# Gated attention with a squared-ReLU MLP: squares, sums and low parts on other engines, a new order of operations in the MLP stage

## The chip, the cores and the metric

The kernel runs on one core of one Trainium2 chip. The metric is the device time of one execution in microseconds (us); lower is better. The core's engines are TensorE (PE, with its weight loads PEld), VectorE (DVE), ScalarE (ACT), GpSimd (POOL) and SyncE (SP, which here only issues DMAs). Each engine takes its own instructions in order and waits for others by semaphores.

## The reference

```python
x = A_x                                # 2048 x 640
xn = _layernorm(x, axis=-1)
s = _A_ref(xn, k_cache, v_cache, wq, wo)   # 32 heads of 128, the last 512 cached keys
g = _silu(_B_ref(xn, w1, b1, w2, b2))      # h = xn @ w1 + b1; r = max(h, 0); (r * r) @ w2 + b2
return x + s * g
```

The MLP's hidden width is 1728, which is 13 chunks of 128 and one of 64 (14 chunks, FC = 14). The model width of 640 is 5 chunks of 128 (DC = 5).

## The kernel before

All products are float32 products made of three TensorE passes: each operand is split into a high part `hi` (a rounded copy, written by ScalarE) and a low part `lo` = operand - hi (a subtraction), and `triple` adds hi\*hi, hi\*lo and lo\*hi into one PSUM bank. So each operand costs one ScalarE copy and one subtraction.

The 2048 tokens are four tiles of 512: tile 0, T1 = 1, T2 = 2 and LATE = 3. Everything is held transposed (model width on the partitions, tokens along the free axis). The program has these stages:

1. **First stage, 14 steps** (`first_step(f)`, about 12 to 118 us). Step f makes hidden chunk f of tile 0 (`up`: 15 matmuls), then its ReLU (ScalarE, `up_end`), its square and split (`square_split`), and then the down product of the chunk before (`down(f - 1)`, 15 matmuls into five PSUM banks). The weights of chunk f come by SP's queue two steps ahead (`load_part`), and are split by `split_w(f, k)`: k = 0 for w1, k = 1 for w2. Beside this, the steps prepare tiles T1 and T2: `ln_load` loads the rows of x, `ln_block` takes their statistics on VectorE, `ln_var` and `ln_root` make mean and reciprocal deviation, `ln_rows` turns them into rows (a TensorE transpose, a VectorE copy, a DMA to DRAM, and two DMAs that broadcast them back into the tiles `mr`), and `ln_chunk(t, c)` loads chunk c of x transposed, subtracts the mean, multiplies, and splits it into the tiles `xT`.
2. **The seven block products** (about 118 to 212 us). The up products of T1 and T2 are made for six pairs of hidden chunks. A pair is a 2 x 2 matrix of blocks (two hidden chunks by two parts of the width), the two tiles are the other one, and Winograd's form needs seven products (`PROD`) instead of eight. `t_sums` makes the sums of x (once), `w_sums(p)` those of the weights of pair p, and `w_split(p, k)` the splits of the weights. `w_first`, `w_second` and `w_third` issue the products of pair p; additions between PSUM banks happen on VectorE (tile `wy` = product sum + p5 in `w_second`, tile `wx` = a + p5 in `w_third`). The fifth chunk of the width is added by `rest`. Each finished chunk goes through `up_end` and `square_out` to DRAM (`h_m`).
3. **The down products of T1 and T2** (`c_load`, `c_prep`, `c_down`, 28 steps), beside which tile LATE is normalised by `ln_chunk`.
4. **Attention** (from about 316 us to the end), whose order is written out by hand with due times, and in which the MLP of tile LATE is placed.

What sets the order: the helper objects `pe`, `dve`, `act`, `pool` and `sp` keep each instruction in program order on its engine, and all of them have line 77 (L77) in the profile. Calls through `nc.vector`, `nc.gpsimd`, `nc.scalar`, `nc.sync` and `nc.tensor` are not kept in order: a planner places them where it expects their inputs to be ready. Such are, in the kernel before, the loads of x (L149, L212), the moves of the rows (L179 to L191), the whole of `ln_chunk` (L213 to L216) and `t_sums` (L535 to L540).

Pools of tiles: `xr` on the right side of SBUF holds `xT` of T1 and the sums `T` of x; `keep` holds `xT` of T2 under the tag acc. The raw weights lie in the tag wr (4 buffers) of pool `mx`, or, for chunks not divisible by three below 9, in acc. Chunks of x lie in the tags stage and mr (2 buffers each) and xb (4). Results of ReLU lie in the tag r (4 buffers).

Of the kernel before, what the change touches and what calls it, by code (L numbers as in the profile page):

```python
# [10 lines left out]
AF = mybir.ActivationFunctionType  # L11
# [14 lines left out]
def kernel(  # L26
# [67 lines left out]
    def raw(ap):  # L94
        return ap.bitcast(F32)
# [105 lines left out]
        ]  # L201

    def ln_chunk(t, c):
        bc, xs = LN[t], XS[t]
        xc = (
            pa.tile([P, D], F32, tag="xb", name=f"xc{t}_{c}", bufs=NB)
            if t == T2 and c in (1, 3)
            else xp.tile(
                [P, D], F32, tag="mr" if t == T2 and c == DC - 1 else "stage", name=f"xc{t}_{c}"
            )  # L210
        )[:, :NT]
        nc.sync.dma_start(xc, xT[c * P : (c + 1) * P, t * NT : (t + 1) * NT])  # L212
        (nc.vector if t == T1 or t == T2 and c > 2 else nc.gpsimd).tensor_tensor(xc, xc, bc[0], op=ALU.subtract)  # L213
        (nc.gpsimd if t == LATE else nc.vector).tensor_tensor(xc, xc, bc[1], op=ALU.mult)
        nc.scalar.activation(xs[0][:, c, :], xc, AF.Copy)
        nc.vector.tensor_tensor(xs[1][:, c, :], xc, raw(xs[0][:, c, :]), op=ALU.subtract)  # L216
        XC[t, c] = xc

    PRE, BOTH, BR = {}, {}, []

# [164 lines left out]
    def split_lo(f, r, k, engine):  # L385
        hi, lo = split_parts(f, k)
        engine.tensor_tensor(lo, r, raw(hi), op=ALU.subtract)

    def split_w(f, k):
        if f < FC:  # L390
            split_hi(f, PRE[f, k], k)
            split_lo(f, PRE[f, k], k, pool if k and 5 <= f < 9 else dve)
            if 8 <= f < FC - 2:
                load_part(f + 2, k)

    def square_split(f, r, hi, lo):
        pool.tensor_tensor(r, r, r, op=ALU.mult)
        if f not in (0, rp, rp + 1) and f < AHEAD_W:
            split_w(f + 1, 0)
        act.activation(hi, r, AF.Copy)  # L400
        dve.tensor_tensor(lo, r, raw(hi), op=ALU.subtract)

    def square_out(t, f, r):
        pool.tensor_tensor(r, r, r, op=ALU.mult)
        sp.dma_start(h_m[t, f][: chunks[f][1], :], r)

    def r_tile(t, f):
# [64 lines left out]

    def up_end(t, f, ph):
        r = r_tile(t, f)
        if t == 0 and f == rp + 1:
# [54 lines left out]
    def t_sums(q):  # L530
        e, o = 2 * q, 2 * q + 1
        (h1, l1), b12, b22 = XS[T1], XC.pop((T2, e)), XC.pop((T2, o))
        t = [tmp(f"ts{q}_{k}") for k in range(4)]
        eng = nc.vector
        eng.tensor_tensor(t[0], b12, raw(h1[:, e, :]), op=ALU.subtract)  # L535
        eng.tensor_tensor(t[0], t[0], raw(l1[:, e, :]), op=ALU.subtract)
        eng.tensor_tensor(t[1], b22, t[0], op=ALU.subtract)
        eng.tensor_tensor(t[2], b22, b12, op=ALU.subtract)
        eng.tensor_tensor(t[3], raw(h1[:, o, :]), t[1], op=ALU.subtract)
        eng.tensor_tensor(t[3], t[3], raw(l1[:, o, :]), op=ALU.add)  # L540
# [19 lines left out]
    def w_sums(p):  # L560
        a, b = WR[p, 0], WR[p, 1]
        a11, a12, a21, a22 = (w[:, k : 2 * NQ2 : 2, :] for w in (a, b) for k in range(2))
        s = [
            (
                tmp(f"ws{p}_{k}")
                if p
                else xp.tile([P, NT], F32, tag="p5", name=f"ws{p}_{k}", bufs=2)
            ).rearrange("p (k q n) -> p k q n", k=2, n=P)
            for k in range(2)
        ]  # L570
        s1, s2, s3, s4 = (w[:, k] for w in s for k in range(2))
        pool.tensor_tensor(s1, a21, a22, op=ALU.add)
        pool.tensor_tensor(s2, s1, a11, op=ALU.subtract)
        pool.tensor_tensor(s3, a11, a21, op=ALU.subtract)
        pool.tensor_tensor(s4, a12, s2, op=ALU.subtract)
        SUMS["w", p] = s

    def wb(tag, shape, name):
# [83 lines left out]
            b[k] = ps_y.tile([P, NT], F32, tag="py", name=f"w{k}{p}")  # L662
        act.activation(b["x"], b["a"], AF.Copy)

    def w_second(p):
        b = PB[p]
        prod(p, 5, b["y"], True)
        b["p5"] = xp.tile([P, NT], F32, tag="p5", name=f"p5_{p}", bufs=2)
        act.activation(b["p5"], b["y"], AF.Copy)
        prod(p, 6, b["a"])  # L670
        dve.tensor_tensor(b["y"], b["a"], b["p5"], op=ALU.add)
        prod(p, 2, b["x"])
        rest(p, 0, 0, b["x"])
        up_end(T1, PAIRS[p][0], b["x"])

    def w_third(p, between=None):
# [12 lines left out]
        up_end(T2, PAIRS[p][1], b["x"])  # L689

    AHEAD_W = 6
    CH = {1: {7: (0, 1), 8: (2, 3), 9: (4,)}, 2: {9: (0,), 10: (1, 2), 11: (3, 4)}}

    def first_step(f):
        if f == 1:
            ln_load(T1)
        if f == 4:
            ln_load(T2)
        if f > 0:
            split_w(f, 1)  # L700
# [5 lines left out]
        for t in (T1, T2):  # L706
            for c in CH[t].get(f, ()):
                if c == 0:
                    open_x(t)
                ln_chunk(t, c)  # L710
# [12 lines left out]
        if f == 12:  # L723
            w_load(0)
        if f == 13:
            w_load(1)
            t_split(1)
        if f == 1:
            PY[0] = [ps_y.tile([P, NT], F32, tag="py", name=f"py0_{d}") for d in range(DC)]
        if f > 0:  # L730
            down(f - 1, home(f - 1, 1), HS.pop(f - 1), PY[0])
        if f == 12:
            t_sums(0)
            t_split(0)
            t_sums(1)

# [457 lines left out]
    down(FC - 1, home(FC - 1, 1), HS.pop(FC - 1), PY[0])  # L1194
    gate(0, gate_tile, range(2))
    up(T1, rp)
    gate(0, gate_tile, (2,))
# [11 lines left out]
    for p in range(1, NP):  # L1209
# [2 lines left out]
            w_load(p + 2)  # L1212
        w_first(p)
        w_seed(p)
        if more:
            w_sums(p + 1)
        w_third(p - 1)
        if more:
            w_split(p + 1, 0)
        else:  # L1220
            for k in range(2):
                c_prep(0, k)
        if p == 1:
            ln_load(LATE)
        if p in (2, 3):
            spill(p - 1, XS[p - 1])
            for b in range(2):
                ln_block(LATE, 2 * (p - 2) + b)
        if p == 3:
            ln_var(LATE)  # L1230
            LN[LATE] = ln_root(LATE)
        if p == NP - 2:
            for m in range(3):
                c_load(m)
        if p == 4:
            LN[LATE] = ln_rows(LATE, LN[LATE])
        w_second(p)
        if more:
            w_split(p + 1, 1)
            w_split(p + 1, 2)  # L1240
    up(T2, FC - 1)
    c_prep(1, 1)
    w_third(NP - 1)
    c_prep(1, 0)
    xctx.close()
    bctx.close()
    for m in range(2 * FC):
# [3 lines left out]
        if m + 2 < 2 * FC:  # L1251
            for k in range(2):
                c_prep(m + 2, k)
        c = m - 2
        if c == 0:
            open_x(LATE)
        if 0 <= c < DC:
            ln_chunk(LATE, c)
        if 0 < c <= DC:
            spill(LATE, XS[LATE], slice(c - 1, c))  # L1260
# [291 lines left out]
```

## Time and profile before

| | |
|---|---|
| time, median of 3 runs | 1977.48 us (1975.9 to 1977.9) |
| time of the profiled execution | 1977.58 us |
| its span | 1975.8 us |
| granted TensorE clock, mean of the span | 0.997 of full speed |
| busy: PE, DVE, POOL, ACT | 99%, 81%, 72%, 62% |
| start of attention's first score products | 316.44 us into the span |

How to read it: the page gives busy times and shares of the whole span, which is mostly attention. The stages that the change touches lie in its first 316 us; there the timeline (instructions in order of time: start, duration, engine, line, operation, `output<-inputs`, count, and in brackets the idle time before it and what ended it) is the view to read. A TensorE row's duration runs to the end of its last matmul and overlaps with the next row by about 0.16 us, so that the length of a group is read from start to start.

### The profile page before, as it was taken

What the parts mean: (1) busy time and instruction counts of PE and PEld (TensorE: products, weight loads), DVE (VectorE), ACT (ScalarE), POOL (GpSimd) and SP (SyncE); (2) the same over time, 40 slices, a digit from 0 to 9 for tenths busy, and PEclk for the clock granted to TensorE, in tenths of its full rate; (3) what the DMA queues carried; (4) which work ended last, traced back from release to release, by engine and by line L of the source; (5) the groups of instructions that cost most, each with busy time, mean ns of one, the idle gap of its engine ahead of it and who ended that gap; (6) DMA issues with size and microseconds to landing.
All of it is one profiled execution on the core that took longest, in us unless ns stands there. A gap on an engine that the chain in (4) does not pass through costs nothing.

```text
span 1975.8 us, 28654 instructions
## 1 busy us (share of the span) xinstructions
PE 1949.8 (99%) x8576; PEld 1605.6 (81%) x8576; DVE 1604.2 (81%) x2717; ACT 1225.4 (62%) x2122; POOL 1426.0 (72%) x798
## 2 busy tenths in 40 slices
PE   9898999999999999999999999999999999999998
PEld 7676887888888888888888888888888888888887
DVE  6865555788888888888888878888888888888864
ACT  5354444766666666666666676666666666666643
POOL 2355503888888888888888888888888888888841
PEclk9899999999999999999999999999999999999999
DMA  6547674333333322232335443433333333322253
GB/s 197 184 149 258 248 259 154 103 91 92 91 92 93 93 93 91 91 92 92 91 92 162 154 120 102 113 114 114 115 115 118 116 117 114 97 92 92 84 187 117
DMA packets 147640, 246.43 MB, mean 125 GB/s; under 512 B 25020, under 2 KB 47334, under 8 KB 146214
## 3 DMA queue, kind: packets, MB, share of 16 engines
q1 hardware_dynamic: 144486, 230.02, 37.3%
q0 software_dynamic: 2864, 14.42, 1.8%
q8 instruction: 77, 1.26, 0.2%
q14 instruction: 69, 0.57, 0.1%
q10 hardware_dynamic: 144, 0.16, 0.0%
HBM read 213.59 MB, written 30.95 MB: 124 GB/s over the span
## 4 chain that ended last, share of the span: by engine, by line
PE 92%; issue 3%; DVE 2%; DMA 1%; ACT 0%; SPq 0%; POOL 0%; ACTq 0%; DVEq 0%; POOLq 0%
PE r L77 22%; PE pq L77 22%; PE s L77 18%; PE o L77 18%; PE py L77 4%; PE ly L77 2%; PE ph L77 2%; PE lu L77 2%; PE wa L77 1%; PE wx L77 1%; PE wy L77 1%; PE eu L77 1%; DMA w1r<-in_w_dram 0%; DVE st L77 0%; DMA mv_d<-lr 0%
## 5 line engine op out<-in xcount | busy, mean ns | idle before, releaser
L77 POOL TENSOR_TENSOR pt<-e,pt 128x1024 fp32r<-128x1024 f32 x256 | 615.4, 2404 | 112.8 <-ACT pt L77 63.6
L77 PE MATMUL r<-ot,wo 128*128 128x512 f32 x1920 | 496.6, 389 | 0.0
L77 PE MATMUL pq<-ax,wq 128*128 128x512 f32 x1920 | 456.1, 389 | 0.0
L77 PEld LDWEIGHTS pq<-ax,wq 128*128 128x128 f32 x1920 | 360.3, 188 | 75.2 <-DVE q L77 0.4
L77 PEld LDWEIGHTS r<-ot,wo 128*128 128x128 f32 x1920 | 360.3, 188 | 74.9
L77 PE MATMUL s<-q,wk 128*128 128x512 f32 x1536 | 369.1, 389 | 0.9 <-DVE sgl L77 0.9
L77 PE MATMUL o<-pt,wv 128*128 128x512 f32 x1536 | 369.2, 389 | 0.0
L77 DVE TRANSPOSE_TENSOR_REDUCE rdm<-s 128x16 f32<-128x512 f32 x512 | 347.3, 712 | 6.2 <-PE s L77 6.1
L77 ACT ACTIVATE e<-e 128x1024 f32<-128x1024 f32 x256 | 269.8, 1054 | 122.1 <-DVE e L77 79.4
L77 PEld LDWEIGHTS s<-q,wk 128*128 128x128 f32 x1536 | 288.2, 188 | 61.2 <-DVE sgl L77 1.3
L77 PEld LDWEIGHTS o<-pt,wv 128*128 128x128 f32 x1536 | 288.2, 188 | 60.3 <-POOL pt L77 0.5
L77 DVE TENSOR_TENSOR e<-s,bm 128x512 f32<-128x512 f32 x512 | 312.1, 664 | 5.1 <-DMA bm<-m_d 4.8
L77 POOL TENSOR_TENSOR su<-e,e 128x1024 f32<-128x1024 f32 x128 | 309.0, 2414 | 0.0
L77 ACT ACTIVATE pt<-e 128x1024 fp32r<-128x1024 f32 x256 | 272.0, 1063 | 6.9
L77 DVE TENSOR_TENSOR acc<-r,acc 128x512 f32<-128x512 f32 x300 | 203.6, 679 | 13.3 <-PE r L77 13.1
L77 ACT ACTIVATE rdm<-rdm 32x64 f32<-32x64 f32 x384 | 97.8, 255 | 184.5 <-DVE rdm L77 181.4
L77 DVE TRANSPOSE_TENSOR_REDUCE rds<-su 128x32 f32<-128x1024 f32 x128 | 158.4, 1237 | 0.3 <-POOL su L77 0.3
L77 DVE TENSOR_TENSOR ot<-o,ot 128x512 fp32r<-128x512 f32 x128 | 88.5, 692 | 86.1 <-ACT ot L77 86.1
L77 ACT ACTIVATE q<-pq 128x512 fp32r<-128x512 f32 x128 | 76.7, 599 | 110.9 <-PE pq L77 110.9
L77 ACT ACTIVATE rds<-rds 32x32 f32<-32x32 f32 x384 | 89.7, 234 | 60.7 <-DVE rds L77 57.4
L77 POOL TENSOR_TENSOR wo<-or,wo 128x640 fp32r<-128x640 f32 x64 | 101.0, 1579 | 30.7 <-ACT wo L77 30.7
L77 POOL TENSOR_TENSOR wv<-vr,wv 128x512 fp32r<-128x512 f32 x64 | 83.3, 1302 | 51.8 <-ACT wv L77 51.8
(176 smaller groups left out, 2078.0 us busy)
## 6 DMA issues: line engine op xcount, KB each, us to landing
bm<-m_d SPq DMA_DIRECT2D x128, 256.0 KB, 3.2
bs<-s_d SPq DMA_DIRECT2D x128, 256.0 KB, 4.0
qr<-in_wq_dram SPq DMA_DIRECT2D x64, 320.0 KB, 4.3
or<-in_wo_dram SPq DMA_DIRECT2D x64, 320.0 KB, 4.8
kr<-in_kT_dram SPq DMA_DIRECT2D x64, 256.0 KB, 4.8
vr<-in_v_dram SPq DMA_DIRECT2D x64, 256.0 KB, 4.4
cw<-in_w_dram SPq DMA_DIRECT2D x26, 320.0 KB, 4.1
xT_d<-xT POOLq DMA_DIRECT2D x6, 1280.0 KB, 5.3
```

What stands on the lines that cost most here:

```text
L77: ins = method(*args, **kwargs)
```

## The change

- **ScalarE takes squares.** The squares of tile 0 (`square_split`) and of T1 (`square_out`) move from GpSimd to ScalarE (`AF.Square`); those of T2 stay on GpSimd.
- **VectorE takes sums and low parts.** `w_sums`, the w2 low parts of chunks 5 to 8, and the subtraction and multiplication of all chunks of x move from GpSimd to VectorE.
- **Order.** `ln_chunk`, its split (new `ln_split`) and `t_sums` are kept in program order. One or two chunks of x are prepared per step from step 6 on, interleaved with the weight splits. The w1 split of the next chunk stands first in the step from step 4 on (AHEAD_W 4 instead of 6). The rows of T1 and T2 are made one and two steps earlier, T2 is loaded one step earlier, `t_sums(0)` runs a step earlier.
- **Blocks.** Product 5 is taken out of `w_second` (new `w_fifth`) and put between products 3 and 4 of the pair before. `w_sums` of the next pair follows its first split. The gate of tile 0's third chunk comes after the first product.
- **LATE.** Its statistics take one block of rows per pair instead of two in pairs 2 and 3, its rows are made one pair later, and its chunks are prepared in every second down step.
- **Pool.** A pad of 480 bytes is added to `xr`, which moves the tiles in it.

```diff
     def ln_chunk(t, c):
+        if c == 0:
+            open_x(t)
...
-        (nc.vector if t == T1 or t == T2 and c > 2 else nc.gpsimd).tensor_tensor(xc, xc, bc[0], op=ALU.subtract)
-        (nc.gpsimd if t == LATE else nc.vector).tensor_tensor(xc, xc, bc[1], op=ALU.mult)
-        nc.scalar.activation(xs[0][:, c, :], xc, AF.Copy)
-        nc.vector.tensor_tensor(xs[1][:, c, :], xc, raw(xs[0][:, c, :]), op=ALU.subtract)
+        dve.tensor_tensor(xc, xc, bc[0], op=ALU.subtract)
+        dve.tensor_tensor(xc, xc, bc[1], op=ALU.mult)
         XC[t, c] = xc
+
+    def ln_split(t, c, k):
+        xc, xs = XC[t, c], XS[t]
+        if k == 0:
+            act.activation(xs[0][:, c, :], xc, AF.Copy)
+        else:
+            dve.tensor_tensor(xs[1][:, c, :], xc, raw(xs[0][:, c, :]), op=ALU.subtract)
...
-    def split_w(f, k):
+    def split_w(f, k, between=None):
         if f < FC:
             split_hi(f, PRE[f, k], k)
-            split_lo(f, PRE[f, k], k, pool if k and 5 <= f < 9 else dve)
+        if between:
+            between()
+        if f < FC:
+            split_lo(f, PRE[f, k], k, dve)
...
     def square_split(f, r, hi, lo):
-        pool.tensor_tensor(r, r, r, op=ALU.mult)
+        act.activation(r, r, AF.Square)
...
     def square_out(t, f, r):
-        pool.tensor_tensor(r, r, r, op=ALU.mult)
+        if t == T1:
+            act.activation(r, r, AF.Square)
+        else:
+            pool.tensor_tensor(r, r, r, op=ALU.mult)
...
+                if k == 3:
+                    pad(xr, 480)
...
-        pool.tensor_tensor(s1, a21, a22, op=ALU.add)
-        pool.tensor_tensor(s2, s1, a11, op=ALU.subtract)
-        pool.tensor_tensor(s3, a11, a21, op=ALU.subtract)
-        pool.tensor_tensor(s4, a12, s2, op=ALU.subtract)
+        dve.tensor_tensor(s1, a21, a22, op=ALU.add)
+        dve.tensor_tensor(s2, s1, a11, op=ALU.subtract)
+        dve.tensor_tensor(s3, a11, a21, op=ALU.subtract)
+        dve.tensor_tensor(s4, a12, s2, op=ALU.subtract)
...
-    def w_second(p):
+    def w_fifth(p):
         b = PB[p]
         prod(p, 5, b["y"], True)
         b["p5"] = xp.tile([P, NT], F32, tag="p5", name=f"p5_{p}", bufs=2)
         act.activation(b["p5"], b["y"], AF.Copy)
+
+    def w_second(p):
+        b = PB[p]
         prod(p, 6, b["a"])
...
         up_end(T2, PAIRS[p][0], b["y"])
+        if middle:
+            middle()
         prod(p, 4, b["a"])
...
-    AHEAD_W = 6
-    CH = {1: {7: (0, 1), 8: (2, 3), 9: (4,)}, 2: {9: (0,), 10: (1, 2), 11: (3, 4)}}
+    AHEAD_W = 4
+    CH_FIRST = {7: (T1, 1), 8: (T1, 3), 9: (T2, 0), 10: (T2, 2), 11: (T2, 4)}
+    CH_SECOND = {6: (T1, 0), 7: (T1, 2), 8: (T1, 4), 9: (T2, 1), 10: (T2, 3)}
...
-        if f == 4:
+        if f == 3:
             ln_load(T2)
+        one, two = (at_.get(f) for at_ in (CH_FIRST, CH_SECOND))
+        if one:
+            ln_chunk(*one)
+        if f >= AHEAD_W:
+            split_w(f + 1, 0, lambda: one and ln_split(*one, 0))
+        if one:
+            ln_split(*one, 1)
+        if two:
+            ln_chunk(*two)
         if f > 0:
             split_w(f, 1)
...
-            if f >= AHEAD_W:
-                split_w(f + 1, 0)
...
         HS[f] = up(0, f)
-        for t, at_ in ((T1, 2), (T2, 5)):
+        if two:
+            for k in range(2):
+                ln_split(*two, k)
+        for t, at_ in ((T1, 2), (T2, 4)):
...
-            if f == at_ + 3:
-                LN[t] = ln_rows(t, LN[t])
...
             down(f - 1, home(f - 1, 1), HS.pop(f - 1), PY[0])
+        for t, at_ in ((T1, 4), (T2, 6)):
+            if f == at_:
+                LN[t] = ln_rows(t, LN[t])
+        if f == 11:
+            t_sums(0)
...
     w_first(0)
     w_seed(0)
+    gate(0, gate_tile, (2,))
     up(T2, rp)
     w_load(2)
     w_sums(1)
     w_split(1, 0)
+    w_fifth(0)
     w_second(0)
...
-        if more:
-            w_sums(p + 1)
-        w_third(p - 1)
-        if more:
-            w_split(p + 1, 0)
-        else:
-            for k in range(2):
-                c_prep(0, k)
+
+        def prepare():
+            if more:
+                w_split(p + 1, 0)
+                w_sums(p + 1)
+            else:
+                for k in range(2):
+                    c_prep(0, k)
+
+        w_third(p - 1, prepare, lambda: w_fifth(p))
...
-            for b in range(2):
-                ln_block(LATE, 2 * (p - 2) + b)
-        if p == 3:
+        if 1 <= p <= NB:
+            ln_block(LATE, p - 1)
+        if p == NB:
             ln_var(LATE)
             LN[LATE] = ln_root(LATE)
...
-        if p == 4:
+        if p == NP - 1:
             LN[LATE] = ln_rows(LATE, LN[LATE])
...
-    c_prep(1, 1)
-    w_third(NP - 1)
-    c_prep(1, 0)
+    w_third(NP - 1, lambda: c_prep(1, 0), lambda: c_prep(1, 1))
```

More of the change, by code (lines that the diff above doesn't have):

```diff
@@ L474, in up_end @@
         r = r_tile(t, f)
-        if t == 0 and f == rp + 1:
+        if t == 0 and AHEAD_W > f == rp + 1:
             split_w(f + 1, 0)
@@ L533, in t_sums @@
         t = [tmp(f"ts{q}_{k}") for k in range(4)]
[L534 to L540, printed above, removed]
+        dve.tensor_tensor(t[0], b12, raw(h1[:, e, :]), op=ALU.subtract)
+        dve.tensor_tensor(t[0], t[0], raw(l1[:, e, :]), op=ALU.subtract)
+        dve.tensor_tensor(t[1], b22, t[0], op=ALU.subtract)
+        dve.tensor_tensor(t[2], b22, b12, op=ALU.subtract)
+        dve.tensor_tensor(t[3], raw(h1[:, o, :]), t[1], op=ALU.subtract)
+        dve.tensor_tensor(t[3], t[3], raw(l1[:, o, :]), op=ALU.add)
         SUMS["t", q] = t
@@ L674, in w_second, with w_third @@
         up_end(T1, PAIRS[p][0], b["x"])
-    def w_third(p, between=None):
+    def w_third(p, between=None, middle=None):
         b = PB.pop(p)
@@ L703, in first_step @@
                     load_part(f + 2, k)
-            if f >= AHEAD_W:
-                split_w(f + 1, 0)
[L706 to L710, printed above, removed]
         HS[f] = up(0, f)
-        for t, at_ in ((T1, 2), (T2, 5)):
+        if two:
+            for k in range(2):
+                ln_split(*two, k)
+        for t, at_ in ((T1, 2), (T2, 4)):
             if f in (at_, at_ + 1):
@@ L731, in first_step @@
             down(f - 1, home(f - 1, 1), HS.pop(f - 1), PY[0])
+        for t, at_ in ((T1, 4), (T2, 6)):
[3 more added lines that the diff above has]
+            t_sums(0)
         if f == 12:
-            t_sums(0)
             t_split(0)
@@ L1196 @@
     up(T1, rp)
-    gate(0, gate_tile, (2,))
     w_first(0)
     w_seed(0)
+    gate(0, gate_tile, (2,))
     up(T2, rp)
@@ L1253 @@
                 c_prep(m + 2, k)
[L1254 to L1260, printed above, removed]
+        c, odd = divmod(m - 2, 2)
+        if not odd:
+            if 0 <= c < DC:
+                ln_chunk(LATE, c)
+                for k in range(2):
+                    ln_split(LATE, c, k)
+            if 0 < c <= DC:
+                spill(LATE, XS[LATE], slice(c - 1, c))
         if m == OPEN:
```

## The prediction

> **What bounds the kernel now.** First the page's busy times, then TensorE's waits.
>
> ```profile
> span 1975.8 us, 28654 instructions
> PE 1949.8 (99%) x8576; PEld 1605.6 (81%) x8576; DVE 1604.2 (81%) x2717; ACT 1225.4 (62%) x2122; POOL 1426.0 (72%) x798
> ```
> ```profile
> PE wa L77 <- DVE wx L77: 5.8, 4, 1.8
> PE ph L77 <- DVE w1s L77: 2.3, 2, 1.8
> PE py L77 <- ACT cw L77: 1.2, 1, 1.2
> PE s L77 <- DVE sgl L77: 0.9, 1, 0.9
> ```
>
> TensorE is the bound: it idles 26 us of 1975.8. The change removes no matmul, so it can win only what TensorE waits or runs slowly, and nearly all of that lies in the stages it touches: the names wa, py, ph are the MLP's banks. So the third view is TensorE's timeline there. In the first stage (start, duration; idle time before in brackets):
>
> ```profile
> 40.61 0.67 PE L77 MATMUL ph<-xT,w1s 128*128 128x512 f32 x2
> 44.87 3.65 PE L77 MATMUL py<-h,w2s 128*128 128x512 f32 x15
> 61.96 0.61 PE L77 MATMUL ph<-xT,w1s 128*128 128x512 f32 x2
> 67.52 3.67 PE L77 MATMUL py<-h,w2s 128*128 128x512 f32 x15
> 77.97 3.56 PE L77 MATMUL ph<-xT,w1s 128*128 128x512 f32 x15
> 85.45 0.79 PE L77 MATMUL py<-h,w2s 128*128 128x512 f32 x1 [3.93 <-ACT h L77]
> 87.96 6.17 PE L77 MATMUL py<-h,w2s 128*128 128x512 f32 x14 [1.71 <-DVE h L77]
> 93.97 3.61 PE L77 MATMUL ph<-xT,w1s 128*128 128x512 f32 x15
> ```
> ```profile
> 100.98 3.40 PE ph L77 x15
> ```
> ```profile
> 80.00:90.00 10.00, 4.36 (x13) 2.88 (x12) 9.73 (x11) 4.12 (x7) 4.73 (x5) 0.68 0.50 192
> ```
>
> The second fence is the chain of waits: a group of 15 matmuls without a wait takes 3.40 us, a step 6.80. The third is a window: over 80 to 90 us the granted clock is 0.68, so that the wait at 85 us costs twice, as idle time and as 14 matmuls in 6.17 us. Lost, start to start: 44.87 - 40.61 - 3.43 = 0.83 (a transpose of 0.03 lies in it); 67.52 - 61.96 - 3.43 = 2.13; 93.97 - 77.97 - 6.80 = 9.20. Together 12.16 us.
>
> In the block products and behind them:
>
> ```profile
> 140.95 1.56 PE L77 MATMUL wy<-T,ws 128*128 128x512 f32 x6
> 155.51 1.56 PE L77 MATMUL wy<-T,ws 128*128 128x512 f32 x6
> 163.21 1.53 PE L77 MATMUL wy<-xT,ws 128*128 128x512 f32 x6
> 167.18 1.66 PE L77 MATMUL wa<-T,wc 128*128 128x512 f32 x6 [1.76 <-DVE wx L77]
> 185.29 1.63 PE L77 MATMUL wy<-T,ws 128*128 128x512 f32 x6
> 197.91 1.56 PE L77 MATMUL wy<-T,ws 128*128 128x512 f32 x6
> 212.51 3.80 PE L77 MATMUL py<-ch,cw 128*128 128x512 f32 x16
> 216.95 86.53 PE L77 MATMUL py<-ch,cw 128*128 128x512 f32 x379 [0.63 <-DVE ch L77]
> ```
>
> The rows of wy are product 5 of successive pairs. The last period, without a wait, is 12.62 us; from 140.95 to 185.29 there are three, 44.34 us, which is 6.48 too many. The first pair's wait for wx is 0.9 more (the waits' sum of 5.8 less three of 1.6 to 1.8, and its restart): 7.4. Behind them the first down step takes 4.44 in place of 3.40: 1.04.
>
> **The change part by part.** *First stage.* Why the waits arise:
>
> ```profile
> 65.48 2.05 DVE L77 TENSOR_TENSOR h<-r,h 128x512 fp32r<-128x512 f32 x1
> 71.07 0.29 SPq L183 DMA_DIRECT2D mv_d<-lr  x1
> 74.40 0.80 SPq L191 DMA_DIRECT2D mr<-mv_d  x2
> 78.46 3.03 POOL L213 TENSOR_TENSOR xc<-xc,mr 128x512 f32<-128x512 f32 x2 [5.25 <-DMA mr<-mv_d]
> ```
> ```profile
> L77 ACT ACTIVATE h<-r 128x512 fp32r<-128x512 f32 x13 | 8.2, 631 | 12.6 <-POOL r L77 12.6
> L77 DVE TENSOR_TENSOR w2s<-wr,w2s 128x640 fp32r<-128x640 f32 x3 | 2.5, 825 | 0.0
> L77 ACT ACT_TABLE_LOAD x5 | 6.4, 1283 | 1.3 <-PEq L1535 1.2
> L164 ACT ACT_TABLE_LOAD x1 | 1.3, 1283 | 0.0
> ```
>
> T2's rows of means (mr) landed at 78.4, 7.3 us behind their first DMA (71.07); until 81.5 GpSimd worked on the chunks of x that had waited for them, and the square of h, GpSimd's too, came behind: 13 copies of h waited 12.6 us for squares. A VectorE subtraction like the last row but two, 0.8 at 640 columns, takes 2.05 at 512 while GpSimd works. The change makes T2's rows two steps earlier, some 12 us (transpose near 55, in place of just ahead of the row at 67.52): with the same 3.6 us from transpose to DMA and 7.3 to landing they are there by 66; the first chunk needs them in step 9, near 69. T1's transpose moves from 44.8 to 40.6; with the same 10.9 us at worst its rows are there by 51.5, when step 6 takes its first chunk; 2 us more would delay only low parts that TensorE needs 4 us later. The broadcasts and the DMA before them pass SP's queue earlier too, where SP waits 3.3 us for the first to land (71.07 to 74.40); queued behind are weights of two steps on, so one step, 6.8 us, covers it. T2's load one step earlier goes into buffers unused till then: nothing.
>
> VectorE's work per step with a chunk of x at both places: two weight parts of 0.82, h 0.69 and six chunk operations of 0.69 (as wx below), 6.5 of 6.80; starts overlap by some 0.08 us, so about 5.8. It fits, barely, and GpSimd no longer computes beside it. ScalarE gets the square. No row shows Square; the copy of h (0.63) is the nearest, and a square costing anything from 0.5 to a copy with a table load (1.9) replaces about one us on GpSimd (12.6 / 13) with two handovers. Per step ScalarE does about seven operations of 0.6 to 0.7, 4.6 us. From the end of an up group h is whole after ReLU, square, copy (0.6 to 0.7 each) and subtraction, about 2.9 us with handovers, and TensorE needs it 6.8 us after: 3.9 of slack. Steps 11 and 12 with the sums of x hold 12 and 13 VectorE operations (7.5 and 8.2 us at overlapped cost), and step 13 has 3.8: the backlog of 2 us is inside the slack. The wait for w1s at 41 goes, since that split now precedes the w2 split on VectorE. I take back all 12.2 us; between 6 and 12.2 if the loads of x wait.
>
> *Block products.* The wait:
>
> ```profile
> 122.04 1.28 DVE L77 TENSOR_TENSOR ws<-ws,ws 128x512 fp32r<-128x512 f32 x2
> 161.90 2.26 DVE L77 TENSOR_TENSOR ws<-ws,ws 128x512 fp32r<-128x512 f32 x2 [0.85 <-ACT ws L77]
> 162.44 1.18 POOL L77 TENSOR_TENSOR ws<-wp 128x256 f32<-128x256 f32 x1
> 164.96 1.55 DVE L77 TENSOR_TENSOR wl<-wp,wl 128x128 fp32r<-128x128 f32 x2
> 166.44 0.69 DVE L77 TENSOR_TENSOR wx<-wa,p 128x512 f32<-128x512 f32 x1
> ```
>
> Product 4 at 167.18 waits for wx, whose inputs were there when product 3 began (163.21). VectorE was in the low parts: ws 2.26 where it takes 1.28 alone, wl 1.55 for two tiny ones, beside GpSimd's sums. With the sums on VectorE behind wx, ws to wl take about 2.2 in place of 4.6; from 161.90, with 0.6 for the square now ahead on ScalarE, they end at 164.7 and wx at 165.4. Product 4 follows product 3, its rest (together nine matmuls, 2.05) and now product 5 (six, 1.4), so at 166.7: 1.3 us to spare where wx was 1.8 late. The sums cost VectorE four operations of 128x256, 0.4 to 0.7 each (half of a 512 one to a whole), in a period in which it is busy about 7 of 12.6 us. Against this speaks a rule. The Trainium skill's page SBUF — State Buffer (section Who interferes with whom) says that a VectorE operation with two SBUF inputs and a GpSimd one that reads SBUF exclude each other, and the stretched rows here agree. By it the squares of T2, still on GpSimd, can each block VectorE for one square; if both of a pair fell ahead of wx, 2 us against 1.3, each of five pairs would lose 0.7 or more, and the sum would be smaller by about 4, 1960.
>
> New waits: product 5 starts 4.2 us earlier in its pair and needs the low part of ws. Counted from product 1 (160.4, two products ahead of 163.21), ws starts at 1.5, with the square at 2.1, and ends at 3.4; product 5 comes after three products and a rest, at 4.9: 1.5 to spare. For the first pair, whose gates stand ahead on ScalarE, nothing is left: 0 to 0.5. LATE's root (a table load of 1.28 in front of its Sqrt) moves to pair 4, just ahead of wy: 0 to 0.6. I take 0.5 for both, so 6.9 of the 7.4.
>
> *Down products.* The split that held the second step comes before the last pair's end: 1.0 gained, from 0 (the results of ReLU have two of four buffers free there) to 1.04. LATE's chunks on VectorE: three operations per 6.8 us beside four of 0.7 to 0.8, hidden. The waits for cw and sgl (2.1) stand in untouched code: they stay.
>
> *The pad.*
>
> ```profile
> L77 PE MATMUL wa<-T,ws 128*128 128x512 f32 x72 | 18.8, 397 | 0.6 <-DVE wy L77 0.6
> L77 PE MATMUL wy<-xT,ws 128*128 128x512 f32 x36 | 9.2, 391 | 0.0
> L77 PE MATMUL pq<-ax,wq 128*128 128x512 f32 x1920 | 456.1, 389 | 0.0
> ```
>
> Matmuls that read x from pool xr take 397 ns; those that read T2 from pool keep take 391, and attention's, whose pool has the same 480-byte pad, 389. 25 matmuls of T1's direct chunks and six pairs of 42 read xr: 277, times 5 to 7 ns. I take 1.6 us; bounds 0 (the place is not the cause) and 1.9.
>
> Sum: 12.2 + 6.9 + 1.0 + 1.6 = 21.7. The profiled execution took 1977.58 us, 1.8 over its span and 0.1 over the median of 1977.48; from the median this gives 1955.8 us.
>
> **The rivals.** *Loads of x wait (0.18).* Two buffers turn over T1's chunks: each load waits for the subtraction of two chunks before, and it may hold SP's queue. Speaks for it: with VectorE busy 85% of a step, a load has only some 3 us. Against: TensorE has 3.9 us of slack per step. One wait like that at 85 us, idle time and clock, gives back 6 to 9: 1962 to 1965. *The block wait moves to product 5 (0.06)*: if ws's low parts still take 2.26 and the square costs more than a copy, or T2's squares hold wx up, about 1 us in each of five pairs: 1961. *Square changes tables (0.04).* Copy and ReLU run beside Sqrt, Sigmoid and Exp with six loads in the whole trace; if Square weren't among each table's functions, some eight more loads of 1.28 would stand on ScalarE, mostly in the gates, 5 to 10 us: 1961 to 1966. The page ScalarE: Activation LUTs (section Table sets: the hidden batching unit) of the Trainium skill says that cheap functions are in every set, without naming square there; no row here shows it. *VectorE becomes the bound (0.05), slower.* Place: steps 6 to 12. At 1.13 us per operation (2.26 for two, as beside GpSimd) a step's nine would take 10.2 us, 3.4 over TensorE's 6.80; in seven steps 24 us, which eats the gain: 1979. It decides from 1.1 us per operation. Against: GpSimd computes nothing there any more. *The pad does nothing:* 1957.4, inside the forecast's own range.
>
> **How the numbers follow.** Forecast 0.67, own range 1953 to 1960. The rivals at 1961 to 1966 hold 0.28, the slower one 0.05. The low end is everything gained with no new wait and the pad at 1.9 (22.5 us: 1955.0) and the 2.1 us of the untouched waits also gone, rounded down: 1952.5. Up to 1966 all but the worst of the first rival and the slower one is in. A measurement here tells 0.2%, 4 us, from no change. Faster 0.93, same 0.02, slower 0.05.
>
> **What would show it.** Right: no TensorE wait over 0.5 us between 20 and 200 us, clock 1.00 in every window; attention's first score products start near 295 in place of 316; pairs of 12.3 to 12.6 us; matmuls of T near 390 ns. Wrong: waits of VectorE for xc or mr that reach TensorE, waits for ws at product 5, table loads beyond six, VectorE operations above 0.7 us in steps 6 to 12.

## The result and the profile after

The changed kernel takes 1955.34 us (median of four runs, 1954.95 to 1957.34) against 1977.47 of the kernel before (1975.9 to 1977.9). The ratio is 0.9892, with a 95% interval of 0.9874 to 0.9909: 22 us, or 1.1%, faster. The profiled execution has a span of 1953.3 us, 22.5 less than before.

The page's busy times and then the waits of TensorE (what it waited for; us in total, times, the longest), changed kernel:

```profile
span 1953.3 us, 28587 instructions
PE 1943.1 (99%) x8576; PEld 1605.8 (82%) x8576; DVE 1599.5 (82%) x2758; ACT 1242.6 (64%) x2150; POOL 1348.2 (69%) x729
```
```profile
PE pw L77 <- POOL mv L77: 1.7, 1, 1.7
PE s L77 <- DVE sgl L77: 1.4, 1, 1.4
PE py L77 <- ACT cw L77: 0.7, 1, 0.7
PE px L77 <- ACT xb L77: 0.3, 1, 0.3
```

The waits for wx (5.8 us), for w1s and for h are gone; what is left stands in the warm-up and in code that the change does not touch. GpSimd is busy 78 us less and ScalarE 17 more. VectorE is busy 5 us less, though it does 41 operations more: operations that used to run beside GpSimd's are shorter (the six low parts of wa, for one, took 7.9 us and now take 4.1).

TensorE's timeline of the changed kernel where the prediction showed that of before (start, duration, group, idle time before it in brackets), with the window of 80 to 90 us (busy time of PE, PEld, DVE, ACT, POOL; granted clock; DMA share; GB/s):

```profile
81.79 3.56 PE L77 MATMUL ph<-xT,w1s 128*128 128x512 f32 x15
85.19 3.56 PE L77 MATMUL py<-h,w2s 128*128 128x512 f32 x15
...
108.99 2.46 PE L77 MATMUL ph<-xT,w1s 128*128 128x512 f32 x10
...
136.95 1.52 PE L77 MATMUL wy<-T,ws 128*128 128x512 f32 x6
138.31 1.52 PE L77 MATMUL wa<-T,wc 128*128 128x512 f32 x6
149.19 1.52 PE L77 MATMUL wy<-T,ws 128*128 128x512 f32 x6
...
190.79 9.46 PE L77 MATMUL py<-ch,cw 128*128 128x512 f32 x41
...
284.99 4.12 PE L77 MATMUL py<-ch,cw 128*128 128x512 f32 x15 [0.74 <-ACT cw L77]
...
293.87 2.37 PE L77 MATMUL s<-q,wk 128*128 128x512 f32 x9 [1.36 <-DVE sgl L77]
```
```profile
80.00:90.00 10.00, 10.00 (x46) 8.29 (x45) 8.70 (x14) 6.87 (x12) 0.00 (x0) 1.00 0.46 131
```

Steps follow each other every 6.80 us without a wait at full clock, where the window at this place had 0.68. Stage by stage, start to start: up to T1's up products of the half-wide chunk, which stand just ahead of the first block product (the row at 108.99), 12.34 us are gained; from there to the first down step 81.80 in place of 91.18, which is 9.38; the down steps to attention's first score products 103.08 in place of 103.93, which is 0.85. From there to the end the two kernels take the same time (1659.43 and 1659.36 us). The row of the kernel before that answers to 108.99:

```profile
121.33 2.50 PE L77 MATMUL ph<-xT,w1s 128*128 128x512 f32 x10
```

### The profile page after: what moved, and what is told of

Same layout as the page of the kernel before. It is cut to its first block, busy times and chain, and to the rows that moved or that the text cites. A ratio compares the mean times of both kernels' runs of the same rounds, so it can differ in the third digit from the quotient of the medians.

```text
span 1953.3 us, 28587 instructions
## 1 busy us (share of the span) xinstructions
PE 1943.1 (99%) x8576; PEld 1605.8 (82%) x8576; DVE 1599.5 (82%) x2758; ACT 1242.6 (64%) x2150; POOL 1348.2 (69%) x729
## 4 chain that ended last, share of the span: by engine, by line
PE 97%; DMA 2%; DVE 0%; issue 0%; ACT 0%; SPq 0%; ACTq 0%; POOLq 0%; DVEq 0%
PE r L77 22%; PE pq L77 22%; PE s L77 18%; PE o L77 18%; PE py L77 6%; PE ph L77 2%; PE ly L77 2%; PE wa L77 2%; PE lu L77 2%; PE wy L77 1%; PE wx L77 1%; DMA w1r<-in_w_dram 1%; DMA ch<-h_m 1%; PE eu L77 1%; DMA xb<-in_x_dram 0%; DMA w2r<-in_w_dram 0%
```

## The experiments

Theory at this point: the first stage gained because T2's rows come in time and GpSimd's work is off h's path; the block products because the sums no longer stretch VectorE's low parts; and the pad sets the rate of matmuls that read pool xr. Each run undoes or varies one of these. Numbers are read by stage, since single runs also differ by what the last experiments are about. Each kernel here but the last was run once; the kernel before, run beside them on three occasions, took 1976.3 to 1978.6 us (medians), so that whole times less than 2 us apart say nothing.

**The pad: none, 32 bytes, 224 bytes.**

```diff
                 if k == 3:
-                    pad(xr, 480)
```

> The changed kernel without the pad of 480 bytes; nothing else differs. Theory (the tiles' place sets the rate of matmuls that read x from pool xr): matmuls of T back at 396 to 397 ns, a pair of block products 12.62 us in place of 12.24, TensorE's first score products 2 to 2.5 us later than 293.87, span about 1955.6 in place of 1953.3. Rival (the higher rate came with the quieter GpSimd): pairs stay at 12.24 and the span at 1953.3.

```diff
-                    pad(xr, 480)
+                    pad(xr, 32)
```

> The changed kernel with a pad of 32 bytes in place of 480, so that the tiles of xr start at a multiple of 64 bytes but not at one of 512. If starts that are no multiple of 64 bytes cost the 7 ns: pairs of 12.24 us, span 1953.3, as with the pad of 480. If a multiple of 512 is wanted: pairs of 12.62 us and span near 1955.6, as without a pad.

```diff
-                    pad(xr, 480)
+                    pad(xr, 224)
```

> The changed kernel with a pad of 224 bytes, so that the tiles of xr start 256 bytes past a multiple of 512 (480 past it without a pad, 448 with 32 bytes, 0 with 480). If only a multiple of 512 gives the full rate: matmuls of T at 394 to 397 ns and pairs of 12.53 to 12.57 us, as in the two runs with other pads. If a multiple of 256 is enough: 390 ns and 12.24 us.

The groups by line (operation, count, busy us, mean ns), products 6 and 7, in the order: changed kernel, without pad, 32 bytes, 224 bytes:

```profile
L77 PE MATMUL wa<-T,ws 128*128 128x512 f32 x72 | 18.4, 390 | 0.0
```
```profile
L77 PE MATMUL wa<-T,ws 128*128 128x512 f32 x72 | 18.8, 397 | 0.0
```
```profile
L77 PE MATMUL wa<-T,ws 128*128 128x512 f32 x72 | 18.8, 396 | 0.0
```
```profile
L77 PE MATMUL wa<-T,ws 128*128 128x512 f32 x72 | 18.4, 390 | 0.0
```

The period of a pair is 12.24 us in the changed kernel and with 224 bytes, 12.53 without a pad (12.62 was expected; see the account of the prediction) and 12.57 with 32 bytes. Between the kernel without a pad, the one with 32 bytes and the changed one, only the ten tiles of xr have other addresses. So the place is the cause, as predicted: 0.29 us a pair, and 0.10 in T1's 15 direct matmuls (a group of 3.50 us without the pad, 3.40 with it). From the row at 110.80 us, which answers to 108.99, to the first down step the kernel without a pad took 83.41 us, 1.61 more. 448 and 480 bytes past a multiple of 512 are slow, 0 and 256 fast: a multiple of 512 is not needed, and one of 64 is not enough. What lies between was not tried. The kernel without a pad ended 6.1 us later in all; beside these 1.7, another 1.7 came up to 30 us (below), 0.8 in the down steps, and 1.9 in attention. Attention's tiles have not moved; 1.6 of the 1.9 are its first two groups of products, which ran under a granted clock of 0.79 (298 to 306 us) behind a wait of 2.04 us for sgl.

**The block products: sums, order, squares.** Three edits could have removed the wait for wx. First one at a time:

```diff
-        dve.tensor_tensor(s1, a21, a22, op=ALU.add)
+        pool.tensor_tensor(s1, a21, a22, op=ALU.add)
...
```

> The changed kernel with the sums of the weights back on GpSimd. Theory: their four operations stretch VectorE's low parts as in the kernel before (2.26 and 1.55 us for what takes 1.28 and about 0.8), some 2 us a pair, against a margin of 1.37 us of wx ahead of product 4: TensorE waits for wx 0.5 to 1.2 us in each of five pairs, span 1956 to 1960. Rival (the new place of product 5 alone covers it): no wait for wx, pairs 12.24, span 1953.3.

```diff
-        w_third(p - 1, prepare, lambda: w_fifth(p))
+        w_third(p - 1, prepare)
...
+        w_fifth(p)
         w_second(p)
```

> The changed kernel with product 5 back at the head of the pair's second half; the sums stay on VectorE. Theory (VectorE's own work is what mattered): without product 5 between, product 4 starts 1.4 us earlier, which the margin of wx (1.37 us) just covers: 0 to 0.1 us a pair, span 1953.3 to 1954. Rival (the order removed the wait): TensorE waits for wx 1 us or more in each of five pairs, span 1958 to 1962.

With the sums on GpSimd TensorE waited for wx once, 0.44 us in the first pair, and all later pairs had 12.24 us: the rival was right but for the first pair. With product 5 at its old place the first pair waited 1.16 us and the others had 12.44, 0.2 more (the weight loads of product 4 stood 0.30 us for wx): neither the theory's 0 to 0.1 nor the rival's 1 us and more. Both small; so both together:

> Sums of the weights back on GpSimd and product 5 back at the head of the pair's second half, both at once. Either alone cost little (first pair apart, 0 and 0.2 us a pair). Theory (each gives wx about 1.4 us, so either is enough, and only both undone bring the wait back): TensorE waits for wx 0.8 to 1.8 us in each of five pairs, pairs 13.2 to 14.2 us in place of 12.24, first score products 5 to 9 us later than 293.87. Rival (another part of the change, such as T1's squares on ScalarE, removed the wait): pairs 12.4 to 12.5, at most 2 us in all.

Again the theory fell. The first pair waited 2.84 us, the rest kept 12.44. The reason stands in the timelines. GpSimd and VectorE in one pair of this run:

```profile
147.67 0.75 POOL L77 TENSOR_TENSOR ws<-wp 128x256 f32<-128x256 f32 x1
...
149.89 0.74 POOL L77 TENSOR_TENSOR ws<-wp,ws 128x256 f32<-128x256 f32 x1
```
```profile
150.91 1.29 DVE L77 TENSOR_TENSOR ws<-ws,ws 128x512 fp32r<-128x512 f32 x2 [3.18 <-ACT ws L77]
```

The sums are over when the low parts begin, and so the low parts take 1.29 us, not 2.26. Before, the sums began at 162.44, behind T1's square on the same engine, and so beside the low parts:

```profile
161.44 1.04 POOL L77 TENSOR_TENSOR r<-r 128x512 f32<-128x512 f32 x1 [2.50 <-ACT r L77]
```

That square is on ScalarE now. New theory: the square's move alone takes the sums out of the low parts' way, after the first pair. So that square went back too, on top of the two:

```diff
     def square_out(t, f, r):
-        if t == T1:
-            act.activation(r, r, AF.Square)
-        else:
-            pool.tensor_tensor(r, r, r, op=ALU.mult)
+        pool.tensor_tensor(r, r, r, op=ALU.mult)
```

> As the kernel with sums on GpSimd and product 5 at the old place, and T1's squares (those of the block products only) back on GpSimd as well. In the kernel before, T1's square at 161.44 us held the sums behind it on GpSimd until 162.44, beside the low parts of ws on VectorE (161.90); with that square on ScalarE the sums began at 147.67 and were over at 150.6, before the low parts of that pair (150.91). Theory (each of three edits parts the sums from the low parts, so only all three undone bring the wait back): TensorE waits for wx 1.4 to 1.9 us in most of the pairs after the first, pairs 13.8 to 14.3 us, score products 7 to 11 us later than 293.87. Rival (the place of the next pair's split or LATE's statistics did it): pairs stay at 12.4 to 12.5, at most 4 us in all, the first pair included.

Waits of TensorE, GpSimd, VectorE and TensorE in this run:

```profile
PE wa L77 <- DVE wx L77: 7.8, 4, 2.3
```
```profile
153.09 1.04 POOL L77 TENSOR_TENSOR r<-r 128x512 f32<-128x512 f32 x1 [3.02 <-ACT r L77]
154.09 1.17 POOL L77 TENSOR_TENSOR ws<-wp 128x256 f32<-128x256 f32 x1
```
```profile
153.55 2.26 DVE L77 TENSOR_TENSOR ws<-ws,ws 128x512 fp32r<-128x512 f32 x2 [2.56 <-ACT ws L77]
...
156.61 1.55 DVE L77 TENSOR_TENSOR wl<-wp,wl 128x128 fp32r<-128x128 f32 x2
```
```profile
158.82 1.65 PE L77 MATMUL wa<-T,wc 128*128 128x512 f32 x6 [1.84 <-DVE wx L77]
```

The old picture is back: square, sums behind it, low parts of 2.26 and 1.55 us as before, a wait of 1.84 where it was 1.76. Four pairs waited, 7.8 us; the first took 16.4 us, the next three 14.4 to 15.7, and the stage 93.84 us in place of 81.80. That is 12.0 us more, and the score products stand 13.1 us later, beyond the expected 7 to 11: behind the two first waits, of 2.28 and 1.84 us, the granted clock was 0.83 (126 to 136 us) and 0.86 (136 to 148). The last pair, which makes no sums for a next one, took 12.26. So the mechanism is the overlap of GpSimd's work, T1's square and then the sums, with the low parts. Undone alone, none of the three edits brings it back (for the squares, the run further down); with T1's square on ScalarE alone it is gone after the first pair. The sums' move or the new order as the only edit was not tried. The Trainium skill's page SBUF — State Buffer (section Who interferes with whom) says that a GpSimd operation reading SBUF and a VectorE one with two SBUF inputs exclude each other; the rows above agree with it.

**The first stage: rows, squares, VectorE's room.**

```diff
-        for t, at_ in ((T1, 4), (T2, 6)):
+        for t, at_ in ((T1, 5), (T2, 8)):
             if f == at_:
                 LN[t] = ln_rows(t, LN[t])
```

(ahead of `down` in place of behind it)

> The rows of means of T1 and T2 made in steps 5 and 8, ahead of the down products, as in the kernel before; all else as changed. Theory: T2's rows land near 75.5 us; the first chunk of T2 stands at the head of step 9 and holds VectorE in order until then, with the split of the next weights behind it, so TensorE waits for w1s of step 10 about 3 us (74.7 to 77.7) and loses up to 3 more to the clock: 3 to 6 us in all, next to nothing for T1. Rival (GpSimd's work on the chunks was the whole cause, the rows' place does not matter): no wait between 40 and 100 us.

VectorE, TensorE and the window of 80 to 90 us of this run:

```profile
77.12 0.69 DVE L77 TENSOR_TENSOR xc<-xc,mr 128x512 f32<-128x512 f32 x1 [5.19 <-DMA mr<-mv_d]
78.48 0.69 DVE L77 TENSOR_TENSOR xc<-xc,mr 128x512 f32<-128x512 f32 x1 [0.67 <-DMA mr<-mv_d]
```
```profile
79.97 4.84 PE L77 MATMUL ph<-xT,w1s 128*128 128x512 f32 x13 [2.80 <-DVE w1s L77]
```
```profile
80.00:90.00 10.00, 10.00 (x37) 8.07 (x38) 9.89 (x16) 7.71 (x13) 0.00 (x0) 0.83 0.39 104
```

VectorE stood 5.9 us for rows that came at 77 and 78.5, and the weights of step 10 behind it were late by 2.80; the 13 matmuls after that took 4.84 us, and the clock's mean over 80 to 90 us was 0.83. The stage ended 6.3 us later than in the changed kernel, of which 1.4 lie at 30 us: 4.9 for the rows, inside the 3 to 6 expected. With `ln_chunk` in program order the early rows are a condition, not a help.

```diff
     def square_split(f, r, hi, lo):
-        act.activation(r, r, AF.Square)
+        pool.tensor_tensor(r, r, r, op=ALU.mult)
...
     def square_out(t, f, r):
-        if t == T1:
-            act.activation(r, r, AF.Square)
-        else:
-            pool.tensor_tensor(r, r, r, op=ALU.mult)
+        pool.tensor_tensor(r, r, r, op=ALU.mult)
```

> All squares back on GpSimd, all else as changed. Theory: in the first stage a square of about 1.0 us replaces 0.63 us on ScalarE and stretches VectorE by up to 1 us a step, inside the slack: no wait, 0 to 1 us; in the block products two more squares a pair stand beside VectorE, 0 to 0.3 us a pair. In all 0 to 3 us. Rival (the squares on GpSimd were what starved h): waits for h in steps 6 to 12 of 3 us or more, with a clock below 1.00.

The score products came 2.7 us later. One wait of 1.15 us stands in the first stage, for the last weights, which VectorE split behind the first sums of x. VectorE reached them 4 us later than in the changed kernel (96.08 for 92.04). In the steps before, one operation on a chunk of x per step met a square and took 0.8 us longer; the last such meeting, GpSimd and then VectorE, and the late split:

```profile
92.76 1.53 POOL L77 TENSOR_TENSOR r<-r 128x512 f32<-128x512 f32 x1 [2.81 <-ACT r L77]
```
```profile
93.31 1.53 DVE L77 TENSOR_TENSOR ts<-xc,xc 128x512 f32<-128x512 f32 x1
...
96.08 0.82 DVE L77 TENSOR_TENSOR w1s<-w1r,w1s 128x640 fp32r<-128x640 f32 x1
```

An operation of 0.69 us takes 1.53 beside a square. The first stage lost 1.3 us where 0 to 1 and no wait were expected, since VectorE has less slack than the theory gave it; the block products lost another 1.3, all in the first pair, and the later pairs kept 12.24. The sum lies in the expected 0 to 3. So the squares on ScalarE bring 2.7 us in this run, not the bulk, as long as the chunks of x are off GpSimd. Putting the chunks back on GpSimd, or all of the first stage's edits at once, was not tried; how the rest of the 12.2 us is shared stays open.

```diff
         HS[f] = up(0, f)
+        if 6 <= f <= 10:
+            e = tmp(f"extra{f}")
+            dve.memset(e, 1.0)
+            for _ in range(4):
+                dve.tensor_tensor(e, e, e, op=ALU.mult)
```

> The changed kernel with five more VectorE operations on a spare tile of 128x512 in each of steps 6 to 10 (one fill, four multiplications of a tile by itself), about 3.1 us a step. Theory (VectorE is used for about 5.8 of 6.80 us a step, with 3.9 us of slack of h behind it): 2.1 us a step too much, 10.5 in five steps, less the slack: TensorE waits 5 to 8 us in all between 65 and 100 us, and with the clock up to 4 more; the rival that VectorE becomes the bound is then a matter of operations that much longer. Rival (more room than I reckoned): under 3 us.

TensorE's waits in this run, and its window of 80 to 100 us:

```profile
PE ph L77 <- DVE w1s L77: 7.4, 6, 2.2
...
PE py L77 <- DVE h L77: 0.8, 1, 0.8
```
```profile
80.00:100.00 20.00, 16.48 (x64) 12.51 (x62) 19.44 (x30) 8.50 (x14) 0.00 (x0) 0.91 0.28 79
```

TensorE waited 8.2 us in the first stage, 0.3 of them at 30 us; the other 7.9, between 65 and 109 us, are the top of the expected 5 to 8. With the clock (0.91) the stage ended 13.2 us later. VectorE was busy 19.44 of 20 us: here it is the bound. Of some 15 us of added work 13.2 came out in the time, so there was a little less room than reckoned; the changed kernel's window of 80 to 90 us has VectorE busy 8.70 of 10 us.

**The DMAs of an emptied engine.** In several of these runs TensorE waited at 30 us for w1s of chunk 3 (the half-wide one; the expectation below calls it the third, and it is the fourth to be computed), which the prediction did not foresee. GpSimd's queue shows why. Its timeline in the kernel before, and then in the changed one:

```profile
84.68 0.74 POOL L77 DMA_DIRECT2D xT_d<-xT  x1
```
```profile
15.20 1.27 POOL L77 DMA_DIRECT2D xT_d<-xT  x2
```

The two DMAs that write tile 0's x out stand in steps 9 and 10 of the program. GpSimd used to reach the first of them behind ten squares; now nothing stands in front, and 2.6 MB go out at 15 us, among the loads of the first weights. To hold them back:

```diff
-        if f in (9, 10):
-            pool.dma_start(xT_d[0][f - 9], raw(XS[0][f - 9]))
+        if f in (11, 12):
+            hold = xp.tile([P, 2, 6], F32, tag="st", name=f"hold{f}", bufs=4)
+            pool.tensor_copy(hold[:, 0, :1], raw(HS[f - 1][0])[:, :1])
+            pool.dma_start(xT_d[0][f - 11], raw(XS[0][f - 11]))
```

> The two DMAs that write tile 0's x to DRAM, on GpSimd's queue, wait for the h of steps 10 and 11 (a copy of one column stands in front of each on GpSimd); all else as changed. In the changed kernel they go out at 15.2 us, since GpSimd has nothing else to do by then, where they went out at 84.7 and 95.0 before. Theory: their 2.6 MB slow the weights' loads; without them the load of the third chunk's w1 lands in time, the up products of that chunk start at 28.9 us (29.16 in the changed kernel's trace, 29.6 to 30.9 in the four runs before this one, with waits of 0.5 to 1.6 us for w1s), and the score products near 293.5. Rival (the loads of x for T1 and T2 slow the weights): the wait for w1s stays between 0.3 and 1.6 us.

SyncE's issues of weights and ScalarE's first split of that chunk, in the run without a pad (the worst) and in this one:

```profile
19.24 9.82 SPq L77 DMA_DIRECT2D wr<-in_w_dram  x4
...
29.80 0.47 ACT L77 ACTIVATE w1s<-w1r 128x320 fp32r<-128x320 f32 x1 [2.58 <-DMA w1r<-in_w_dram]
```
```profile
20.15 4.97 SPq L77 DMA_DIRECT2D wr<-in_w_dram  x4
...
28.04 0.45 ACT L77 ACTIVATE w1s<-w1r 128x320 fp32r<-128x320 f32 x1
```

The wait for w1s is gone. (The row stands at 29.98 in place of the expected 28.9, because in this run the loads of the first x came 1 us later; from the group before it 3.40 us pass, where the changed kernel has 3.70 and the run without a pad 5.19.) For that reason the score products stand at 294.17, not near 293.5, and as a whole this run is no faster than the changed kernel (1955.59 us). The thirteen kernels with the change fall into two groups by this. In the three that write late (this one, the one with all squares on GpSimd, whose squares hold the DMAs back, and the last one below) the four issues take 4.30 to 4.97 us and ScalarE does not wait for the load. In the ten that write early they take 7.78 to 9.82, ScalarE waits 0.48 to 2.58, and TensorE loses 0 to 1.8.

**A further version.** Besides this hold, it loads the last down step's operands four positions earlier, and gives the last gate tile of T2 its own buffer:

```diff
-        if m + 3 < 2 * FC:
+        if m + 3 < 2 * FC - 1:
             c_load(m + 3)
...
+        if m == OPEN + 2:
+            c_load(2 * FC - 1)
...
-        lambda d: pools["ep"].tile([P, NT], F32, tag=f"wv{d % 2}", name=f"sgl{d}", bufs=G),
+        lambda d: pools["ep"].tile([P, NT], F32, tag="q1", name=f"sgl{d}", bufs=AHEAD + 1)
+        if d == DC - 1
+        else pools["ep"].tile([P, NT], F32, tag=f"wv{d % 2}", name=f"sgl{d}", bufs=G),
```

> The changed kernel with three further edits: tile 0's x is written to DRAM in steps 11 and 12 instead of at 15 us; the loads of the last down step's weights and h go out four positions earlier, ahead of the loads of attention's x; the gate's fifth tile of T2 gets a buffer of its own. Theory: the waits for w1s at 30 us (0 to 1.6 us over the runs), for cw at 285 us (0.4 to 1.1, and 0.55 for the slower restart) and for sgl at 294 us (1.0 to 2.0) go: score products near 291, span 1950 to 1951.5, time 1952 to 1953.5 us, ratio to the kernel before 0.987 to 0.988. Rival (a wait at sgl moves to the next thing that is late, the split of attention's first weights): score products near 292.5, time 1954.

TensorE's waits, all of them, and the row of the first score products:

```profile
PE pw L77 <- POOL mv L77: 1.7, 1, 1.7
PE px L77 <- ACT xb L77: 1.1, 2, 0.8
```
```profile
291.04 2.88 PE L77 MATMUL s<-q,wk 128*128 128x512 f32 x12
```

1951.79 us (1951.58 to 1952.84, four runs; 1952 to 1953.5 was expected) against 1976.32 of the kernel before; ratio 0.9878, interval 0.9862 to 0.9895. From 13 us to the score products TensorE waits for nothing, and these start at 291.04. Its four times lie below all four of the changed kernel (1954.95 at least), but the two ratios' intervals overlap, so the gain of about 3 us over the changed kernel rests on the trace: both late waits, 2.1 us, and the slow restart of the last down step are gone.

## Why the prediction was right, step by step

The forecast was 1955.8 us; 1955.34 was measured.

**First stage, 12.2 taken back.** Measured 12.34, of which 0.1 is the pad in T1's direct matmuls. No load of x stopped TensorE. VectorE waited for chunks three times, which cost TensorE nothing: the longest time for T1's chunk 3, the last for T2's first chunk (VectorE's timeline, changed kernel; then SyncE's queue):

```profile
64.09 1.42 DVE L77 TENSOR_TENSOR xc<-xc,mr 128x512 f32<-128x512 f32 x2 [2.52 <-DMA xc<-in_xT_dram]
...
70.74 1.42 DVE L77 TENSOR_TENSOR xc<-xc,mr 128x512 f32<-128x512 f32 x2 [0.57 <-DMA xc<-in_xT_dram]
```
```profile
58.38 0.80 SPq L191 DMA_DIRECT2D mr<-mv_d  x2
```

T2's rows go out at 58.38 us, and such a broadcast took 3.5 to 5.2 us to land, so they are there by 64.4 at the latest (the step claimed 66); at 70.74 VectorE waits for the chunk, not for them. That they decide is shown by the run with late rows, 4.9 us. The squares are worth another 1.3 in this stage; which edit brings the rest of the 12.2 was not shown. VectorE's use was put at 5.8 of 6.80 us a step, and the window of 80 to 90 us gives 5.9. The slower rival did not come: the added load shows that VectorE becomes the bound when a step holds 3 us more, but in the changed kernel the chunk operations took 0.69 us, not 1.1.

**T2's load, the broadcasts, the queues: nothing.** This step missed a queue. It followed the DMAs that the change moves, and not those that an emptied GpSimd issues 70 us earlier. In the profiled run they cost 0.3 us at chunk 3 (3.70 for 3.40 us), in others up to 1.8. That the sum for the stage came out even so is luck: its start came 0.4 us earlier in this run.

**Square on ScalarE.** It took 633 ns, as the copy that stood in for it, and the table loads stayed at six, so that this rival was wrong. Groups by line, changed kernel:

```profile
L77 ACT ACTIVATE r<-r 128x512 f32<-128x512 f32 (+1 forms) x28 | 17.7, 633 | 0.9
L77 ACT ACT_TABLE_LOAD x5 | 6.4, 1283 | 1.3 <-PEq L1564 1.2
L164 ACT ACT_TABLE_LOAD x1 | 1.3, 1283 | 0.0
```

**Block products, 6.9 of 7.4.** Neither new wait (the first pair's gates, LATE's root) was seen; the first pair took 0.14 us more than the others, at product 4, where 0.5 had been set aside. Measured are 9.38: 1.61 of the pad and 7.77 of waits, where the step had 7.4. Start to start, the four waits for wx had cost 6.90 (1.06 in the first pair, then 2.03, 2.02 and 1.79). The other 0.87 is a wait that the step took for a part of these. TensorE's timeline, kernel before:

```profile
177.13 1.66 PE L77 MATMUL wa<-T,ws 128*128 128x512 f32 x6 [0.61 <-DVE wy L77]
...
185.26 0.27 PE L77 MATMUL pmv<-ident,mv 128*8 128x128 f32 x1
```

At 177 us TensorE waited for wy, which stood on VectorE behind LATE's statistics and root. This wait did not come back in the run with three edits undone, so it does not hang on them; that spreading LATE's statistics removed it fits, but was not tried by itself. The second row is why the step had 7.4 and not 7.77: the period that it took as free of waits, 12.62, holds a transpose, which makes it 0.09 longer than the 12.53 of the kernel without a pad; and the first pair's wait had cost 1.06, not 0.9. The margin of wx is 1.37 us (the row below ends at 136.94, product 4 starts at 138.31), where 1.3 was worked out. VectorE's timeline, changed kernel:

```profile
136.25 0.69 DVE L77 TENSOR_TENSOR wx<-wa,p 128x512 f32<-128x512 f32 x1
```

For the four waits for wx the mechanism, VectorE's low parts beside GpSimd's sums, was right. That the sums' move and product 5's place are what removes it was too narrow: T1's square, which had held the sums back, suffices by its move after the first pair. The rival that the wait moves to product 5 did not come: product 5 at 136.95 waits for nothing. T2's squares do stretch VectorE's sums (1.27 us for 0.42 at 138.24), but behind wx, where it costs nothing.

**Down products, 1.0.** Measured 0.90 up to the last step before attention, and 0.85 up to the score products, since the waits for cw and sgl stayed, as foretold (2.1 us in both traces).

**The pad, 1.6.** Measured 1.7 (1.61 and 0.10). The step took the place for the cause, with a bound of 0 if it is not, and that it is the cause is shown.

**Together** 12.34, 9.38 and 0.85 make 22.57 us against a sum of 21.7. The term that was mis-sized is the block products', 7.77 for 6.9: by the 0.5 set aside for waits that did not come, and by 0.4 for the transpose in the reference period and the first pair's wait. That the median lies within 0.5 us of the forecast is in part luck, since the four runs of the changed kernel alone spread over 2.4 us.

## What to carry to other kernels

When work leaves an engine, look at what stands behind that work on its queue: operations and DMAs start as early as their inputs allow, and here one such shift (sums ahead of low parts) removed a wait and another (2.6 MB of writes among the first loads) made one. A wait caused by two engines' overlap can be removed by several edits at once, and undoing one at a time then shows little. Where equal matmuls differ by some per cent between tiles, compare where the tiles start.

## What the runs showed of the hardware

- A 128x512 float32 matmul whose moving operand starts 448 or 480 bytes past a multiple of 512 took 396 to 397 ns, against 390 at 0 or 256 past it: 1.7% of those products' time.
- A 128x512 VectorE operation on two SBUF tiles took 1.53 us beside a GpSimd square, against 0.69 alone (run with all squares on GpSimd), and one of 128x256 1.27 against 0.42 (changed kernel, at 138 us); the order in which small operations fall decides a wait of 1.84 us.
- After an idle time of 2.80 us (run with late rows) TensorE's granted clock had a mean of 0.83 over the window of 80 to 90 us, which added about 1.7 us (13 matmuls in 4.84 us in place of 3.1). After 2.04 us it was 0.79 over 298 to 306 us (run without a pad), after 1.36 us 1.00 (changed kernel, 293 to 303). After 1.84 us it fell once and once not (run with three edits undone: 0.86 over 136 to 148 us, 1.00 over 158 to 162).
- Two DMAs of 1.28 MB on GpSimd's queue lengthened four issues on SyncE's queue from 4.3 to 5.0 us to 7.8 to 9.8 us.
